# Induced attention with a leaky feed-forward: the feed-forward in 32-row TensorE tiles, four at a time

## The chip, the cores and the metric

One core of one Trainium2 chip. The metric is device microseconds (us) of one execution. Engines: TensorE (PE) multiplies, ScalarE (ACT), VectorE (DVE) and GpSimd (POOL) work elementwise, SyncE (SP) issues DMAs.

## The reference

All in float32; x is 4 x 12480 x 128, the inducing points 32 x 128.

```python
scale = 1.0 / np.sqrt(C)                       # C = 128
def mab(q, kv):
    s = scale * (q @ kv.transpose(0, 2, 1))
    s = s - s.max(-1, keepdims=True)
    a = np.exp(s)
    a /= a.sum(-1, keepdims=True) + 1e-09
    return a @ kv
h = mab(I, x)                                  # 32 inducing points look at a batch's tokens
y = mab(x, h).reshape(49920, 128)              # each token looks at the 32 rows of h
g = y @ w_in                                   # 128 x 2048
g = np.maximum(0.01 * g, g)
out = g @ w_out                                # 2048 x 128
```

## The kernel before, in words

**Algebra.** A token's attention output is a @ h with only 32 weights a, so the first product of the feed-forward is a @ (h @ w_in): it needs a contraction over 32 rows, not 128. The leaky part is split: max(0.01 g, g) = 0.99 relu(g) + 0.01 g, and the second term is linear, a @ (h @ w_in @ w_out) times 0.01. So per batch there is an expanded weight `hws` (h @ w_in, 32 x 2048, times 0.99) and a small `m2s` (the linear part, 32 x 128).

**Precision.** TensorE runs the feed-forward on the F32R type, and each operand is split into a high part and the rest (hi, lo). The 128 rows of one first product hold the four combinations of attention weights and expanded weights, 32 rows each: `A4` has ahi, alo, ahi, alo in its row groups, `hws` hi, hi, lo, lo. The second product sums over 128 of the 2048 hidden columns and takes three matmuls: ghi by w_hi, glo by w_hi, ghi by w_lo.

**Tiles and slots.** Tokens are cut into NT = 98 tiles: 24 of 512 columns per batch, and two of 384 that hold the rests of two batches each. A tile has NF = 16 slots f, one per 128 hidden columns. A slot is `ffn_first` (one matmul into a `ph` bank, L813; the relu on ACT that gives `ghi`, L821; the subtraction on DVE that gives `glo`, L823) and `ffn_second` (three matmuls into the tile's accumulator `po`, L841). The last slot adds the linear part (L847). `ffn_first` runs LOOK = 3 slots ahead. At a tile's end `store` transposes the accumulator from PSUM to SBUF on DVE (L857), and SP issues its stores (L868).

**PSUM.** Eight banks: three for `ph` and other general work, two for accumulators and the first batch's transposes, one for `h_ps`, two for the other lanes (`aux`).

**The other lanes.** The attention of the next batch runs between the slots, a few steps per slot, in an order written by hand: `first_scores` (s_ps, L305; mx_ps, L334), `first_values` with `accumulate` (h_ps, L425), `normalise`, `expand_weights` (hw_ps, L617 for the first batch, L624 for others, whose parts SP spreads over the row groups with 16 copies), `expand_linear`, then `second` (each token's weights; its two elementwise steps on POOL, L675 and L689) and `stack`, which splits them (ahi L715 on ACT, alo L720 on POOL) and lets SP copy them into the four row groups of `A4` (L732, four copies per tile). `debt` and HEAVY keep the lanes' DVE work apart. s_ps, h_ps and the later batches' hw_ps use column tiles: four matmuls of 32 output columns each, side by side. The first two tiles take their weights from `quick` and alternate in rounds of TURN = 4 slots.

## Time and profile before

| | |
|---|---|
| time, median of 3 runs | 1618.82 us (1618.67 to 1618.82) |
| span of the profiled execution | 1616.3 us |
| what lies around the span | 2.5 us, the median less the span; the profiled execution's own time is given by its span only |
| PE busy | 1598.8 us, 99% |
| DVE busy | 1289.1 us, 80% |
| ACT busy | 1009.8 us, 62% |
| POOL busy | 99.7 us, 6% |
| HBM | 48.94 MB read, 25.56 MB written |

A line of the profile that names a group of instructions has: line of the kernel, engine, operation, what is written and read, shapes and count; then busy us and mean ns of one; then the idle time of the engine before it and what ended it. Matmul durations overlap, since they are pipelined; the distance from start to start tells their price. A matmul in plain F32 makes two records.

### The profile page before, as it was taken

The page shows a single profiled execution, that of the slowest core. Times are in us where ns is not written, and L with a number is a line of the kernel's source. Part 1 is how long each engine was busy: PE and PEld are TensorE (multiplying, and loading weights), DVE is VectorE, ACT ScalarE, POOL GpSimd, SP SyncE. Part 2 cuts the span into 40 slices and gives each one's busy share as a digit, 9 for nine tenths or more (in the row PEclk, how much of TensorE's full clock was granted, in tenths as well). Part 3 has the DMA queues.
Part 4 walks back from the last instruction along what each step waited for, and adds up shares of the span by engine and source line. Part 5 has one row for each costly group of instructions (what it writes and reads, how often), then busy time and mean ns, then how long its engine had stood idle before and what let it go on. Part 6 is the DMA issues. An engine that isn't in the chain of part 4 may idle for free.

```text
span 1616.3 us, 22589 instructions
## 1 busy us (share of the span) xinstructions
PE 1598.8 (99%) x7967; PEld 1256.3 (78%) x7967; DVE 1289.1 (80%) x2245; ACT 1009.8 (62%) x1770; POOL 99.7 (6%) x100
## 2 busy tenths in 40 slices
PE   7999999999999999999999999999999999999998
PEld 5677777777778777777777777777777788888886
DVE  6778878877888888787878888877878777777776
ACT  6566666656666666566666666656666666666665
POOL 2110010000100100000011000000101000000000
PEclk9999999999999999999999999999999999999999
DMA  7142233532334245421224244531211111211211
GB/s 264 24 106 47 56 83 72 102 71 45 66 66 77 49 86 108 96 65 39 43 47 94 50 78 102 110 73 39 61 29 35 35 30 40 43 24 41 43 22 20
DMA packets 401313, 104.21 MB, mean 64 GB/s; under 512 B 372368, under 2 KB 374832, under 8 KB 401200
## 3 DMA queue, kind: packets, MB, share of 16 engines
q1 hardware_dynamic: 400096, 102.62, 30.6%
q8 instruction: 63, 1.03, 0.3%
q14 instruction: 50, 0.41, 0.1%
q10 hardware_dynamic: 1104, 0.15, 0.1%
HBM read 48.94 MB, written 25.56 MB: 46 GB/s over the span
## 4 chain that ended last, share of the span: by engine, by line
PE 97%; DMA 1%; DVE 1%; SPq 0%; ACT 0%; issue 0%; DVEq 0%; ACTq 0%
PE po L841 67%; PE ph L813 23%; PE s_ps L305 3%; PE po L847 1%; PE h_ps L425 1%; DMA xr<-in_x_dram 1%; DMA raw<-in_moe_w_in_dram 1%; PE w_ps L259 0%; SPq L513 0%; PE mx_ps L334 0%; PE hw_ps L617 0%; PE hw_ps L624 0%; PE xT_ps L538 0%; DVE glo L823 0%; PE m_ps L648 0%
## 5 line engine op out<-in xcount | busy, mean ns | idle before, releaser
L823 DVE SCALAR_TENSOR_TENSOR glo<-ph,ghi 128x512 fp32r<-128x512 f32 (+1 forms) x1568 | 1051.8, 681 | 300.1 <-ACT ghi L821 294.6
L821 ACT ACTIVATE ghi<-ph 128x512 fp32r<-128x512 f32 (+1 forms) x1568 | 933.9, 597 | 571.1 <-PE ph L813 569.4
L813 PE MATMUL ph<-A,hws 128*128 128x512 f32 (+1 forms) x1600 | 623.1, 393 | 1.5 <-DVE glo L823 1.5
L841 PE MATMUL po<-ghi,w_hi 128*128 128x512 f32 (+1 forms) x1568 | 618.1, 394 | 0.0
L841 PE MATMUL po<-glo,w_hi 128*128 128x512 f32 (+1 forms) x1568 | 616.8, 393 | 0.0
L841 PE MATMUL po<-ghi,w_lo 128*128 128x512 f32 (+1 forms) x1568 | 613.4, 391 | 0.0
L813 PEld LDWEIGHTS ph<-A,hws 128*128 128x128 f32 x1600 | 299.9, 188 | 92.1 <-DVE glo L823 14.7
L841 PEld LDWEIGHTS po<-ghi,w_lo 128*128 128x128 f32 x1568 | 294.3, 188 | 70.0
L841 PEld LDWEIGHTS po<-glo,w_hi 128*128 128x128 f32 x1568 | 294.4, 188 | 66.4
L841 PEld LDWEIGHTS po<-ghi,w_hi 128*128 128x128 f32 x1568 | 294.4, 188 | 61.1 <-issue 0.2
L720 POOL TENSOR_TENSOR alo<-aT,ahi 128x512 fp32r<-128x512 f32 x24 | 31.2, 1298 | 704.6 <-ACT ahi L715 701.9
L857 DVE STREAM_TRANSPOSE osb<-po 128x512 f32<-128x512 f32 (+1 forms) x98 | 68.9, 703 | 1.7 <-PE po L847 1.7
L675 POOL TENSOR_TENSOR y<-y,mx 128x512 f32<-128x512 f32 (+1 forms) x27 | 25.4, 940 | 458.3 <-DVE mx L673 458.3
L406 DVE STREAM_TRANSPOSE xT<-xc 128x512 f32<-128x512 f32 x72 | 50.5, 702 | 0.0
L847 PE MATMUL po<-A,m2s 128*128 128x512 f32 (+1 forms) x100 | 38.6, 389 | 0.0
L689 POOL TENSOR_TENSOR y<-y,sm 128x512 f32<-128x512 f32 (+1 forms) x27 | 25.4, 939 | 186.6 <-DVE sm L687 103.0
L425 PEld LDWEIGHTS h_ps<-xr,ay 128*32 128x32 f32 (+1 forms) x784 | 22.0, 110 | 12.8 <-issue 12.1
L425 PE MATMUL h_ps<-xr,ay 128*32 128x128 f32 (+1 forms) x784 | 27.2, 274 | 0.4 <-DVE zg L356 0.3
L305 PE MATMUL s_ps<-xT,indT 128*32 128x512 f32 x192 | 26.3, 622 | 1.2 <-ACT xT L544 1.2
L305 PE MATMUL s_ps<-xT,hT 128*32 128x512 f32 x192 | 25.6, 605 | 0.0
L317 DVE TENSOR_SCALAR_CACHE_REDUCE e<-s_ps 128x512 f32<-128x512 f32 (+1 forms) x28 | 17.1, 611 | 8.0 <-PE s_ps L305 7.7
L847 PEld LDWEIGHTS po<-A,m2s 128*128 128x128 f32 x100 | 18.7, 187 | 4.3
(111 smaller groups left out, 385.9 us busy)
## 6 DMA issues: line engine op xcount, KB each, us to landing
xr<-in_x_dram SPq DMA_DIRECT2D x96, 256.0 KB, 4.5
out_dram<-osb SPq DMA_DIRECT2D x382, 64.0 KB, 2.2
xc<-in_x_dram SPq DMA_DIRECT2D x288, 64.0 KB, 2.7
A<-ahi SPq DMA_DIRECT2D x188, 64.0 KB, 2.0
A<-alo SPq DMA_DIRECT2D x188, 64.0 KB, 2.0
raw<-in_moe_w_in_dram SPq DMA_DIRECT2D x4, 512.0 KB, 6.6
raw<-in_moe_w_out_dram SPq DMA_DIRECT2D x4, 512.0 KB, 7.2
hws<-hwhi SPq DMA_DIRECT2D x24, 64.0 KB, 2.0
```

The lines of the kernel that those rows point to most:

```text
L305: nc.tensor.matmul(dst, lhsT, rhs, start=True, stop=True)
L406: nc.vector.transpose(t[:, j, :], blk.rearrange("p n c -> p (n c)"))
L425: nc.tensor.matmul(hp[32 * k : 32 * k + 32, :C], ay[:rows, 4 * q + k, :], xb[:rows, k, :], start=(q == 0), stop=(4 * q + 4 >= K), tile_pos ...
L675: eng.tensor_tensor(out=yv, in0=yv, in1=mx[:rows, :K].unsqueeze(2).broadcast_to([rows, K, M]), op=ALU.subtract,)
L689: eng.tensor_tensor(out=yv, in0=yv, in1=smv.unsqueeze(2).broadcast_to([rows, K, M]), op=ALU.mult)
L720: (eng or nc.gpsimd).tensor_tensor(out=alo[sl], in0=aT.pop((b, g))[: 32 * J, :], in1=ahi[sl].bitcast(F32), op=ALU.subtract,)
L813: nc.tensor.matmul(ph[:, o : o + w], hw[b][1][:, f * P : (f + 1) * P], A4[t][:, o : o + w], start=True, stop=True,)
L821: nc.scalar.activation(ghi[:, :n], ph[:, :n], AF.Relu)
L823: nc.vector.scalar_tensor_tensor(out=glo[:, :n], in0=ph[:, :n], scalar=0.0, in1=ghi[:, :n].bitcast(F32), op0=ALU.max, op1=ALU.subtract,)
L841: nc.tensor.matmul(po[:, :n], w[:, f, :], r[:, :n], start=(f == 0 and r is ghi and w is w_hi), stop=False)
L847: nc.tensor.matmul(po[:, o : o + w], hw[b][2], a4[:, o : o + w], start=False, stop=(o + w == n),)
L857: nc.vector.transpose(osb[:, :n], po[:, :n])
```

## The change

In a middle phase, from tile 2 to the last but one, every matmul of the feed-forward is cut into quarters of 32 rows, each in its own row group of the array and into a PSUM bank of its own. Four generators, `row_group(0)` to `row_group(3)`, take turns, one quarter matmul each.

- A slot's first product is now three quarters (hi by hi, lo by hi, hi by lo) in row group f % 4, after one another into one `ph` bank. `A4` holds ahi and alo in two planes, each copied into all four row groups (eight copies per tile); the expanded weights stay as `expand_weights` leaves them, hidden columns f in row group f % 4, so their spreading by copies goes. The linear part takes three quarters in three of the row groups.
- A second product's three matmuls become twelve quarters, three in each row group. Each row group has its own accumulator bank, and runs LAG = 1 slot behind the one before.
- `gather` adds the four partial sums: ACT copies those of row groups 0 and 2 into SBUF, DVE adds 1 and 3 to them, POOL adds the two. `store` transposes the sum from SBUF.
- Where f % 4 is 3 (FAR), the relu goes to SBUF on ACT, and POOL makes `ghi` (a copy) and `glo` (a subtraction); its first product runs eight slots ahead, the others four. DVE's `glo` is emitted LATER = 4 turns after the relu.
- The eight banks are one pool (`bank`, `done`); in the middle phase the one that is expected free first is taken. A4_BUFS goes from 6 to 3 (of twice the size), XR from 16 to 9, the output buffers from 3 to 2.
- The lanes yield ON_PE ahead of their matmuls and are let go together by `cluster`; in the first four slots of a tile (QUIET) no lane but the stores moves. HEAVY is 2.
- The first two tiles and the last go as before with a full-array second product; their first products are four at a time, in a round of four slots (`first_round`).

```diff
-    HEAVY = 3
+    HEAVY = 2
+    FAR = 3
+    XB = 3
+    QUIET = range(4)
+    LATER = 4
+    FURTHER = 4
+    ON_PE = "pe"
...
-    A4_BUFS = 6
-    XR = 16
+    A4_BUFS = 3
+    XR = 9
+    GB = 7
+    AHEAD = 4
+    LAG = 1
...
-    ps_h = ctx.enter_context(tc.tile_pool(name="ps_h", bufs=LOOK, space=bass.MemoryType.PSUM))
-    ps_o = ctx.enter_context(tc.tile_pool(name="ps_o", bufs=2, space=bass.MemoryType.PSUM))
-    ps_s = ctx.enter_context(tc.tile_pool(name="ps_s", bufs=1, space=bass.MemoryType.PSUM))
-    ps_a = ctx.enter_context(tc.tile_pool(name="ps_a", bufs=2, space=bass.MemoryType.PSUM))
+    ps = ctx.enter_context(tc.tile_pool(name="ps", bufs=1, space=bass.MemoryType.PSUM))
+    banks = [ps.tile([P, TOK], F32, tag=f"bank{i}", name=f"bank{i}") for i in range(8)]
+    turns = {"gen": [0, 1, 2], "out": [3, 4], "hp": [5], "aux": [6, 7]}
+    quads = [False]
+    held, free = set(), []
+
+    def bank(kind):
+        if quads[0]:
+            if not free:
+                happen(math.inf)
+            i = free.pop(0)[1]
+        else:
+            i = next(i for i in turns[kind] if i not in held)
+            turns[kind].remove(i)
+            turns[kind].append(i)
+        held.add(i)
+        return banks[i]
+
+    turn = [0]
+
+    def done(t, later=6):
+        i = next(i for i in range(8) if banks[i] is t)
+        held.discard(i)
+        if quads[0]:
+            free.append((turn[0] + later, i))
+            free.sort()
...
         yield HEAVY
+        if b:
+            yield ON_PE
...
+        hi = sb.tile([P, TOK + P], F32R, tag="hwhi", name="hwhi", bufs=2)
+        lo = sb.tile([P, TOK + P], F32R, tag="hwlo", name="hwlo", bufs=2)
+        if b:
+            yield ON_PE
+        src_bank[0] = pw = aux_ps("hw_ps")
+        cols = w_in_sb.rearrange("p (q c k) -> p c q k", c=4, k=P)
...
-        for c in range(4):
-            for r in range(4):
-                nc.sync.dma_start(
-                    hws[32 * r : 32 * r + 32, c * TOK : (c + 1) * TOK].bitcast(F32),
-                    (hi, lo)[r // 2][32 * c : 32 * c + 32, :].bitcast(F32),
-                )
-            yield
+        split(hi[:, :TOK], lo[:, :TOK], pw, 1.0 - SLOPE)
+        hw[b][1:3] = hi, lo
+        yield HEAVY
...
+            while len(A4) >= A4_BUFS:
+                yield
+            a4 = sb.tile([P, 2, TOK], F32R, tag="A4", name="A4", bufs=A4_BUFS)
             to = 0
             for b, g, js in parts:
                 w, o = 32 * GROUPS[g][2], at[b, g]
                 for j in js:
-                    for r in range(4):
-                        nc.sync.dma_start(
-                            a4[32 * r : 32 * r + 32, to : to + w].bitcast(F32),
-                            (ahi, alo)[r % 2][32 * j : 32 * j + 32, o : o + w].bitcast(F32),
-                        )
+                    for which in range(2):
+                        for r in range(4):
+                            nc.sync.dma_start(
+                                a4[32 * r : 32 * r + 32, which, to : to + w].bitcast(F32),
+                                (ahi, alo)[which][32 * j : 32 * j + 32, o : o + w].bitcast(F32),
+                            )
                     to += w
-                yield
+                    yield
+            A4[t] = a4
...
+    def split_first(ph, t, f):
+
+        _, n = spans(t)
+        far, bufs = ("x", XB) if f % 4 == FAR else ("", GB)
+        ghi = sb.tile([P, TOK], F32R, tag="ghi" + far, name="ghi", bufs=bufs)
+        glo = sb.tile([P, TOK], F32R, tag="glo" + far, name="glo", bufs=bufs)
+        live[t, f] = (ghi, glo)
+        if quads[0] and f % 4 == FAR:
+            g = sb.tile([P, TOK], F32, tag="g", name="g", bufs=2)
+            nc.scalar.activation(g[:, :n], ph[:, :n], AF.Relu)
+            done(ph, 4)
+            nc.gpsimd.tensor_copy(ghi[:, :n], g[:, :n])
+            nc.gpsimd.tensor_tensor(
+                out=glo[:, :n], in0=g[:, :n], in1=ghi[:, :n].bitcast(F32), op=ALU.subtract
+            )
+            return
+        nc.scalar.activation(ghi[:, :n], ph[:, :n], AF.Relu)
+
+        def rest():
+            nc.vector.scalar_tensor_tensor(
+                out=glo[:, :n],
+                in0=ph[:, :n],
+                scalar=0.0,
+                in1=ghi[:, :n].bitcast(F32),
+                op0=ALU.max,
+                op1=ALU.subtract,
+            )
+            done(ph, 4)
+
+        if quads[0]:
+            events.append((turn[0] + LATER, rest))
+        else:
+            rest()
+
+    events = []
+
+    def happen(upto):
+        while events and events[0][0] <= upto:
+            events.pop(0)[1]()
+
+    def quarter(dst, w, x, r, start, stop):
+        nc.tensor.matmul(
+            dst, w[32 * r : 32 * r + 32], x[32 * r : 32 * r + 32],
+            start=start, stop=stop, tile_position=(32 * r, 0),
+        )
+
...
+    def ffn_first(t, f):
+
         parts, n = spans(t)
+        r, c = f % 4, f // 4 * P
         ph = gen_ps("ph")
         for b, o, w in parts:
-            nc.tensor.matmul(
-                ph[:, o : o + w],
-                hw[b][1][:, f * P : (f + 1) * P],
-                A4[t][:, o : o + w],
-                start=True,
-                stop=True,
-            )
-        ghi = sb.tile([P, TOK], F32R, tag="ghi", name="ghi", bufs=LOOK + 2)
-        nc.scalar.activation(ghi[:, :n], ph[:, :n], AF.Relu)
-        glo = sb.tile([P, TOK], F32R, tag="glo", name="glo", bufs=LOOK + 2)
-        nc.vector.scalar_tensor_tensor(
-            out=glo[:, :n],
-            in0=ph[:, :n],
-            scalar=0.0,
-            in1=ghi[:, :n].bitcast(F32),
-            op0=ALU.max,
-            op1=ALU.subtract,
-        )
-        live[u] = (ghi, glo)
-
-    def ffn_second(u):
-        t, f = slots[u]
+            for k in range(3):
+                wt, a = hw[b][1 + k % 2][:, c : c + P], A4[t][:, k // 2, o : o + w]
+                quarter(ph[:, o : o + w], wt, a, r, k == 0, k == 2)
+                if o + w == n:
+                    yield
+        split_first(ph, t, f)
+
+    def ffn_second(t, f):
+
         parts, n = spans(t)
-        ghi, glo = live.pop(u)
+        ghi, glo = live.pop((t, f))
         if f == 0:
-            accs[t] = ps_o.tile([P, TOK], F32, tag="po", name="po")
+            accs[t] = bank("out")
         po = accs[t]
-        for w, r in ((w_hi, ghi), (w_hi, glo), (w_lo, ghi)):
+        for w, r in ((w_hi, ghi), (w_lo, ghi), (w_hi, glo)):
             nc.tensor.matmul(
                 po[:, :n], w[:, f, :], r[:, :n], start=(f == 0 and r is ghi and w is w_hi), stop=False
             )
-        if f == NF - 1:
-            a4 = A4.pop(t)
-            for b, o, w in parts:
+
...
+    def store(t, total, summed):
+        if summed:
+            yield from idle(3)
+        osb = sb.tile([P, TOK], F32, tag="osb", name="osb", bufs=2)
+        nc.vector.transpose(osb[:, :n], total[:, :n])
+        if summed:
+            unsaved.remove(t)
+        else:
+            done(total)
...
+        def cluster(least):
+            for lane in (values, scores, seconds):
+                for _ in range(2):
+                    if lane and id(lane) in waiting and clock[0] - waiting[id(lane)] >= least:
+                        step(lane, True)
+
+        def next_slot(f=NF):
+            clock[0] += 1
+            debt[0] = max(0, debt[0] - (f in QUIET))
+            if f in QUIET:
+                if f >= 3:
+                    step(stores)
+                return
+            others(clock[0])
+            ages = [clock[0] - a for a in waiting.values()]
+            if ages and (max(ages) >= 10 or len(ages) > 1 and min(ages) >= 3):
+                cluster(2)
+
+        work = [(t, f) for t in range(QUICK, NT - 1) for f in range(NF)]
+
+        def row_group(r):
+
+            todo = []
+            for i, (t, f) in enumerate(work):
+                if f % 4 == r:
+                    todo.append((i - AHEAD - FURTHER * (r == FAR), 0, "first", t, f))
+                todo.append((i + LAG * r, 1, "second", t, f))
+                if r != t % 4 and f == (3 if t > QUICK + 3 else NF - 1):
+                    todo.append((i + LAG * r + 0.5, 2, "linear", t, (r - t) % 4 - 1))
+            todo.sort()
+            left = {}
+            for due_at, _, kind, t, f in todo:
+                while due_at < 8 and turn[0] < (due_at + AHEAD) * 3.75 - 1:
+                    yield
+                parts, n = spans(t)
+                if kind == "first":
+                    if f == 0:
+                        begin(t)
+                    waits = 0
+                    while t not in A4 or any(hw[b][1] is None for b, _, _ in parts):
+                        next_slot()
+                        waits += 1
+                        assert waits < 500, (t, A4.keys(), waiting)
+                    yield from ffn_first(t, f)
+                elif kind == "second":
+                    if f == 0:
+                        accs[t, r] = bank("out")
+                        left[t] = NF + (r != t % 4)
+                    po = accs[t, r]
+                    ghi, glo = live[t, f]
+                    left[t] -= 1
+                    for k, (w, x) in enumerate(((w_hi, ghi), (w_lo, ghi), (w_hi, glo))):
+                        quarter(
+                            po[:, :n], w[:, f, :], x[:, :n], r,
+                            f == 0 and k == 0, not left[t] and k == 2,
+                        )
+                        yield
+                    if r == 3:
+                        del live[t, f]
+                    if r == 0:
+                        next_slot(f)
+                else:
+                    for b, _, _ in parts:
+                        assert hw[b][3]
+                    left[t] -= 1
+                    for b, o, w in parts:
+                        quarter(
+                            accs[t, r][:, o : o + w], hw[b][1 + f % 2][:, TOK:],
+                            A4[t][:, f // 2, o : o + w], r, False, not left[t] and o + w == n,
+                        )
+                    yield
+                if t in left and not left[t]:
+                    del left[t]
+                    gather(t, r)
+
+        def gather(t, r):
+            _, n = spans(t)
+            po = accs.pop((t, r))
+            if r % 2 == 0:
+                while unsaved:
+                    step(stores)
+                parts_of[t, r] = part = sb.tile([P, TOK], F32, tag="part", name="part", bufs=2)
+                nc.scalar.copy(part[:, :n], po[:, :n])
+            else:
+                part = parts_of[t, r - 1]
+                nc.vector.tensor_tensor(out=part[:, :n], in0=po[:, :n], in1=part[:, :n], op=ALU.add)
+            done(po)
+            if r == 3:
+                total, part = parts_of.pop((t, 0)), parts_of.pop((t, 2))
+                nc.gpsimd.tensor_tensor(out=total[:, :n], in0=total[:, :n], in1=part[:, :n], op=ALU.add)
+                unsaved.append(t)
+                stores.append(store(t, total, True))
+                del A4[t]
+
+        streams = [row_group(r) for r in range(4)]
+        while streams:
+            streams = [m for m in streams if next(m, StopIteration) is not StopIteration]
+            turn[0] += 1
+            happen(turn[0])
...
```

More of the change, by code (lines that the diff above doesn't have):

```diff
@@ L608, in expand_weights @@
+    src_bank = [None]
     def expand_weights(b):
         hT = hw[b][0]
-        hws = sb.tile([P, DFF], F32R, tag="hws", name="hws", bufs=2)
-        hw[b][1] = hws
-        if b == 0:
-            for c in range(4):
-                sl = slice(c * TOK, (c + 1) * TOK)
-                pw = ps_s.tile([P, TOK], F32, tag="hp", name="hw_ps")
-                nc.tensor.matmul(pw, hT, w_in_sb[:, sl], start=True, stop=True)
-                yield
-                yield from split(hws[:, sl], pw, TOK, 1.0 - SLOPE)
-                yield from idle(3 if c else 1)
-            return
@@ L654, in second, with expand_linear @@
+        hw[b][1:3] = hi, lo
+        yield HEAVY
+    def expand_linear(b):
+        hT, hi, lo, _ = hw[b]
+        if b:
+            yield ON_PE
+        src_bank[0] = pw = aux_ps("m2_ps")
+        nc.tensor.matmul(pw[:, :P], hT, w12, start=True, stop=True)
+        split(hi[:, TOK:], lo[:, TOK:], pw[:, :P], 1.0)
+        hw[b][3] = True
+        yield
     def second(b, g, eng=None):
@@ L702, in stack @@
     def stack(tiles_, eng=None):
-        while len(A4) + len(tiles_) > A4_BUFS or not all(s[:2] in aT for t in tiles_ for s in t[1]):
+        while not all(s[:2] in aT for t in tiles_ for s in t[1]):
             yield
@@ L752, in quick @@
         nc.vector.tensor_reduce(out=mx, in_=sv, op=ALU.max, axis=AX.X)
[L753 removed]
+        y = sb.tile([P, 4, M], F32, tag=("ahi", "alo")[t], name="qy", bufs=1)
         nc.vector.tensor_tensor(
@@ L766, in quick @@
         yield
-        pa = ps_o.tile([P, TOK], F32, tag="po", name="a4_ps")
+        pa = bank("out")
         for c in range(4):
@@ L886, in idle, with step @@
             yield
-    def step(lane):
-        if lane:
-            got = next(lane[0], StopIteration)
-            if got is StopIteration:
-                lane.pop(0)
-            elif got:
-                debt[0] += got
+    waiting = {}
+    clock = [0]
+    def step(lane, on_pe=False):
+        if not lane or (id(lane) in waiting and not on_pe):
+            return
+        waiting.pop(id(lane), None)
+        got = next(lane[0], StopIteration)
+        while got is ON_PE and not quads[0]:
+            got = next(lane[0], StopIteration)
+        if got is StopIteration:
+            lane.pop(0)
+        elif got is ON_PE:
+            waiting[id(lane)] = clock[0]
+        elif got:
+            debt[0] += got
     def after_h(b):
@@ L923, in induced_attention_then_leaky_ffn, with first_round @@
         for lane in (
-            one, weights, two, one, weights, one, two, weights, one, one, two, two, one, two,
+            one, weights, two, one, one, two, one, one, two, two, one, two,
         ):
             step(lane)
-        ffn_first(0)
-        ffn_first(1)
+        def first_round(t, f0):
+            made = [ffn_first(t, f0 + k) for k in range(TURN)]
+            while made:
+                made = [m for m in made if next(m, StopIteration) is not StopIteration]
+            happen(math.inf)
+        first_round(*rounds[0])
         step(two)
-        ffn_first(2)
         stacks[0] = stacks[0][QUICK:]
@@ L968, in induced_attention_then_leaky_ffn @@
                     step(values)
-                    if b + 1 in hw and not had:
-                        seconds += [second(b + 1, g) for g in [0, 1, RG, 2, 3, 4, 5]]
+            for b in hw:
+                if b not in known:
+                    known.add(b)
+                    seconds.extend(second(b, g) for g in [0, 1, RG, 2, 3, 4, 5])
+        begin(0)
+        u = 0
+        for i, (t, f0) in enumerate(rounds):
+            if i + 1 < len(rounds):
+                first_round(*rounds[i + 1])
+            for f in range(f0, f0 + TURN):
+                ffn_second(t, f)
+                if f == NF - 1:
+                    linear_part(t)
+                    stores.append(store(t, accs.pop(t), False))
+                others(u)
+                u += 1
@@ new lines, in induced_attention_then_leaky_ffn @@
+        while weights or linear:
+            step(weights)
+            step(linear)
+        for lane in (stores,):
+            while len(lane) > 1 or held & {3, 4}:
+                step(lane)
+        quads[0] = True
+        free.extend((0, i) for i in [*range(3), 5, 6, 7, 3, 4] if i not in held)
+        clock[0] = u
+        def cluster(least):
[3 more added lines that the diff above has]
+                        step(lane, True)
@@ L971, in induced_attention_then_leaky_ffn @@
+        linear_part(t)
+        stores.append(store(t, accs.pop(t), False))
         for gen in stores:
```

171 lines of the change are left out of this document (79 added, 92 removed).

## The prediction

> **What bounds the kernel now.** I read the page first: the share of each engine and the chain that ended last.
>
> ```profile
> span 1616.3 us, 22589 instructions
> PE 1598.8 (99%) x7967; PEld 1256.3 (78%) x7967; DVE 1289.1 (80%) x2245; ACT 1009.8 (62%) x1770; POOL 99.7 (6%) x100
> PEclk9999999999999999999999999999999999999999
> PE 97%; DMA 1%; DVE 1%; SPq 0%; ACT 0%; issue 0%; DVEq 0%; ACTq 0%
> L823 DVE SCALAR_TENSOR_TENSOR glo<-ph,ghi 128x512 fp32r<-128x512 f32 (+1 forms) x1568 | 1051.8, 681 | 300.1 <-ACT ghi L821 294.6
> L821 ACT ACTIVATE ghi<-ph 128x512 fp32r<-128x512 f32 (+1 forms) x1568 | 933.9, 597 | 571.1 <-PE ph L813 569.4
> L813 PE MATMUL ph<-A,hws 128*128 128x512 f32 (+1 forms) x1600 | 623.1, 393 | 1.5 <-DVE glo L823 1.5
> ```
>
> TensorE is the bound: 97% of the chain, granted clock full throughout, and the feed-forward's own matmul (L813) waited 1.5 us in all. ACT and DVE are the ones that wait (571 and 300 us). A matmul's 393 ns overlaps its neighbours, so its price is read from start to start, in the timeline of one slot (one of a tile's 16 f):
>
> ```profile
> 803.80 0.40 PE L813 MATMUL ph<-A,hws 128*128 128x512 f32 x1
> 803.80 0.19 PEld L841 LDWEIGHTS po<-ghi,w_hi 128*128 128x128 f32 x1
> 804.03 0.40 PE L841 MATMUL po<-ghi,w_hi 128*128 128x512 f32 x1
> 804.23 0.60 ACT L821 ACTIVATE ghi<-ph 128x512 fp32r<-128x512 f32 x1 [0.33 <-PE ph L813]
> 804.27 0.39 PE L841 MATMUL po<-glo,w_hi 128*128 128x512 f32 x1
> 804.50 0.39 PE L841 MATMUL po<-ghi,w_lo 128*128 128x512 f32 x1
> 804.73 0.39 PE L813 MATMUL ph<-A,hws 128*128 128x512 f32 x1
> 804.87 0.69 DVE L823 SCALAR_TENSOR_TENSOR glo<-ph,ghi 128x512 fp32r<-128x512 f32 x1 [0.24 <-ACT ghi L821]
> ```
>
> Four matmuls in 0.93 us, 0.23 each. The last stage, where hardly anything but the feed-forward runs, gives it exactly; in the chain each tile ends on such a row:
>
> ```profile
> 1324.56 0.70 PE po L841 x3
> ...
> 1595.76 0.70 PE po L841 x3
> ```
>
> Eighteen tiles in 271.2 us: 15.07 us a tile, over 65 matmuls (16 times four, and one linear part) 0.2318 us.
>
> **The change on TensorE.** A slot's first product becomes three products of 32 rows, and the three second products become twelve; a tile's linear part becomes three. That is 16 x 15 + 3 = 243 quarter matmuls, four at a time 60.75 rounds. Whether a round costs one matmul's 0.2318 us is the heart of the forecast. No 32-row tile is in this trace; the nearest rows are the 32-column tiles of an excursion, which also go four at a time:
>
> ```profile
> 264.68 0.40 PE L841 MATMUL po<-ghi,w_lo 128*128 128x512 f32 x1
> 265.00 1.06 PE L305 MATMUL s_ps<-xT,indT 128*32 128x512 f32 x8
> 265.89 1.06 PE L425 MATMUL h_ps<-xr,ay 128*32 128x128 f32 x32
> 265.89 0.79 PEld L425 LDWEIGHTS h_ps<-xr,ay 128*32 128x32 f32 x28 [0.30 <-issue]
> 266.87 0.50 PE L813 MATMUL ph<-A,hws 128*128 128x512 f32 x1
> 267.21 0.39 PE L841 MATMUL po<-ghi,w_hi 128*128 128x512 f32 x1
> L425 PEld LDWEIGHTS h_ps<-xr,ay 128*32 128x32 f32 (+1 forms) x784 | 22.0, 110 | 12.8 <-issue 12.1
> 57.26 1.09 PEld L259 LDWEIGHTS w_ps<-wraw,winT 128*128 128x128 f32 x8
> 57.49 1.05 PE L259 MATMUL w_ps<-wraw,winT 128*128 128x128 f32 x8
> 58.30 0.48 PE L813 MATMUL ph<-A,hws 128*128 128x512 f32 x1
> ```
>
> Eight full-array records of 128 columns (L259) take 0.81 us until the next matmul starts, 0.10 each. Thirty-two quarter records of the same length (L425) take 0.98 us, change of shape included: 0.12 for a round of four. So the four run beside each other, and so do their weight loads: 28 of 110 ns, 3.1 us together, lie within 0.79. Issue is no limit either: 0.98/32 = 31 ns a pair, where a round has 58. I take 0.2318 us a round. Above it the bound is 0.32 (the step into another shape, 264.68 to 265.00, paid in every round); below, a round is no faster than the one matmul it copies. A tile takes 60.75 x 0.2318 = 14.08 us, 0.99 less. 95 tiles of 98 go this way: **-93.6**. The first two and the last compute only their first products in quarters: 12 rounds, 48 full matmuls and 3 lone quarters make 63 steps of 0.2318, 0.46 us less each, against eight changes of shape of about 0.1 each: **+1**.
>
> The Trainium skill, "TensorE: Matmul & The Clock Gate", Part 3 (Measured speedup vs the span model), puts four row tiles of 512 columns at 3.07 times one, not 4. By that a round would cost 4/3.07 x 0.2318 = 0.302 us, a tile 18.3, and the kernel about 1940 us, an estimate. The column tiles above do not bear it out in steady state, and no run here shows row tiles yet.
>
> **Excursions.** Entering another shape costs 0.32 - 0.23 = 0.09 us, leaving it 0.34 - 0.23 = 0.11 (266.87 to 267.21), with some drain besides: 0.3 together. They are paid already around s_ps and h_ps. What is full-array work now pays them newly:
>
> ```profile
> L334 PE MATMUL mx_ps<-rd,e 128*128 128x4 f32 x56 | 8.1, 214 | 1.0 <-DVE rd L329 1.0
> L617 PE MATMUL hw_ps<-w_in_sb,hT 128*128 128x512 f32 x8 | 4.2, 602 | 0.0
> ```
>
> 28 mx_ps (two records each), batch 0's seven before the new phase, and with them z_ps, hT_ps and m_ps, some 30 times, 9 us; gathering the lanes' work into clusters behind ON_PE saves some of the old ones. **+5**, bounds -6 and +9.
>
> **The other engines, by stage.**
>
> ```profile
> 100.00:400.00 300.00, 300.00 (x1516) 233.59 (x1515) 245.38 (x437) 186.36 (x329) 16.50 (x16) 1.00 0.34 68
> 400.00:700.00 300.00, 299.60 (x1482) 236.26 (x1481) 246.45 (x439) 188.40 (x334) 19.26 (x20) 1.00 0.39 78
> 700.00:1000.00 300.00, 300.00 (x1459) 233.70 (x1458) 243.39 (x424) 186.60 (x324) 18.38 (x18) 1.00 0.33 67
> 1000.00:1300.00 300.00, 300.00 (x1455) 235.20 (x1454) 241.01 (x406) 188.90 (x332) 20.30 (x21) 1.00 0.26 53
> L720 POOL TENSOR_TENSOR alo<-aT,ahi 128x512 fp32r<-128x512 f32 x24 | 31.2, 1298 | 704.6 <-ACT ahi L715 701.9
> L675 POOL TENSOR_TENSOR y<-y,mx 128x512 f32<-128x512 f32 x23 | 24.2, 1053 | 394.1 <-DVE mx L673 394.1
> L148 POOL TENSOR_TENSOR w_in_sb<-cv_a,cv_t 128x512 f32<-128x512 f32 x4 | 5.7, 1430 | 23.5 <-DVE cv_t L144 23.5
> ```
>
> The columns after the stretch are PE, PEld, DVE, ACT and POOL busy. The 1200 us hold about 74 tiles of 16.2 us: DVE 13.2 us a tile, ACT 10.1, POOL 1.0.
> - DVE loses a quarter of its glo (4 x 0.68), gains two additions of partial sums, priced like a glo: 11.8 us. It stays below the new period of 15.2: nothing on the path.
> - ACT keeps its 16 relus and gains two copies of a partial sum, priced like a ghi (0.60): 11.3.
> - POOL, nearly idle now, takes every fourth f: a copy (bounds 0.29, the 96x64 y, and 1.43, w_in_sb; I take y's 1.05, the row with the least second input) and a subtraction (alo, 1.30), four times a tile, and the final addition (1.30): 11.7 us with its own, and with 1.43 for all nine 13.9. Below the period even in the last stage (14.1), so hidden; the eight slots (7 us) of lead cover 0.43 + 0.60 + 2.35 and a y queued ahead. If that cover were gone, POOL would set the period.
> - The store is emitted three slots later; its transpose now reads SBUF after POOL's addition. Only the last tile's tail shows, and that tile keeps the old way: 0.
> - SP: a tile's A4 takes eight copies instead of four, one weight spread of 48 copies goes.
>
> ```profile
> L675 POOL TENSOR_TENSOR y<-y,mx 96x64 f32<-96x64 f32 x4 | 1.2, 291 | 64.1 <-DVE mx L673 64.1
> L732 SPq DMA_DIRECT2D A<-ahi x212: 507/582/1368, 81.6 to 1533.9; - x106
> SPq L868 <- DVE glo L823: 480.1, 81, 14.6
> ```
>
> 424 - 48 = 376 more issues of 0.58 us are 218 us of SP's queue. A store that waits for its transpose (480 us now, no load of its own) holds the copies behind it, but three A4 buffers let a tile's copies be issued more than a tile ahead: 0. Only tile 2, the first of the new phase, has no such lead: up to 8 x 0.58 + 2, in the next item.
> - Hand-overs: the four streams start and end once, each a chain of ph, ghi, glo (0.43 + 0.60 + 0.69 and two more rounds, 2.2 us), and the old phase's stores are drained first: **+6** (bounds 2 and 13). Batch 0's four full hw_ps products (L617, 4.2 us busy with their overlaps) become one set of column tiles (0.89, as s_ps): **-1**, bounds 0 and -3.
>
> **What is late next: PSUM banks.** The four partial sums hold four of eight banks, and each keeps its old one while it is read out: 0.43 + 0.60 + 0.3 of queueing, 1.3 us in 14.1, together 4.4 banks. A ph bank is held two rounds longer than now: 0.46 + 0.43 + 0.60 + 0.04 + 0.69 + 0.3 = 2.5 us (1.5 where POOL takes over): 9.0 bank-us in 3.48, 2.6 banks. Mean 7.0 of 8, 7.3 with the other lanes'. But where a tile changes, four banks turn over one slot (0.87 us) apart and 1.5 more are out for about 4 us: 5.5 + 2.6 = 8.1. There TensorE waits, all four streams with it, since its queue is in order. Bounds: nothing, and one whole read-out (1.3 us); nearer the lower end, as the excess is 0.1 of a bank, I take 0.35 us a tile: **+33** (0 to 124).
>
> Sum: -93.6 + 1 + 5 + 6 - 1 + 33 = -49.6, from the span of 1616.3 to 1566.7. The runs shown have a median of 1618.82, 2.5 above that span; so 1569 us.
>
> **Rivals.**
> 1. No wait for banks (15%): other lanes are kept off a tile's first four slots, and releases fall into place. Against it speaks the 8.1. 1536 us.
> 2. The waits eat it (15%): every tile change waits for a read-out that stands in ACT's or DVE's queue behind two relus or glos. ACT is at 74%, DVE at 78% of the new period, which speaks for queueing; today's 1.5 us of waits at 81% DVE speak against. 1.3 us a tile give 1660; it decides from (93.6 - 11)/95 = 0.87 us a tile. Slower in most of it. The Trainium skill, "TensorEngine Tiling (Array Packing)", PSUM Bottleneck, warns the same way: tiling speeds up TensorE, not the read-out.
> 3. Rounds drain (6%): 32-row tiles write four banks at once, which column tiles never do; if each round drained as the change of shape does, 0.32 a round, a tile takes 19.4 and the kernel about 2040. It decides from (93.6 - 44)/95/60.75 = 9 ns a round. The skill's 3.07 would be this case, at its 0.302.
> 4. Weight loads of row tiles go one after another (4%): 128 columns at 0.10 (L259), four in 0.40, a round takes 0.40: a tile 24.3, about 2500. Against it: the 28 loads in 0.79, though of 32 columns each.
>
> **How the numbers follow.** The forecast has 60%, with a range of its own of 1540 to 1605. The change that a measurement here can tell from none is about 0.2% (3 us). Faster: 60 + 15 = 75%; same 4%, slower 11% out of rival 2, with 3 and 4 slower 21%. The range reaches down to 1520 (rival 1 with excursions at their lower bound), up to 1650 into rival 2; outside are 3, 4 and the end of 2, about 17%.
>
> **What will show it.** In the last stage, tiles 14.1 to 14.5 us apart; within a slot, row tiles starting in groups of four 0.23 us apart. Starts 0.30 or 0.40 apart would be rivals 3 or 4. Idle time of TensorE behind ACT's copies of partial sums or DVE's additions, bunched at f = 0 to 3, is the bank term; idle time behind POOL would mean that its price was wrong, and waits for A4's copies that SP was.

## The result: slower by 3.4%, where 3% faster was forecast

| | before | after |
|---|---|---|
| median | 1618.82 us (1618.67 to 1618.83) | 1674.28 us (1673.30 to 1675.05) |
| ratio to before, 95% interval | | 1.0342 [1.0328, 1.0357] |
| profiled execution | span 1616.3 us | 1674.81 us, span 1672.7 us |

The forecast was 1569 us, with a range of 1520 to 1650. The page after, from its shares of engines, its slices, its chain and its groups of instructions:

```profile
span 1672.7 us, 60122 instructions
PE 1562.8 (93%) x25047; PEld 1353.4 (81%) x25047; DVE 1163.7 (70%) x2046; ACT 1066.9 (64%) x1957; POOL 941.7 (56%) x963
PE   8999999999966899999996999999999598999997
PEclk9899999999977999999998999999999799999998
PE 79%; SPq 11%; DMA 3%; DVE 3%; issue 2%; POOL 1%; ACT 1%; ACTq 0%; DVEq 0%; POOLq 0%
L874 PE MATMUL bank<-ghi,w_hi 32*128 32x512 f32 x6080 | 1295.8, 394 | 0.6 <-DVE part L1157 0.4
L874 PE MATMUL bank<-A,hwhi 32*128 32x512 f32 (+1 forms) x3394 | 1136.0, 394 | 68.1 <-ACT g L842 62.4
L844 POOL CAST ghi<-g 128x512 fp32r<-128x512 f32 (+1 forms) x384 | 234.1, 610 | 407.1 <-ACT g L842 339.2
L845 POOL TENSOR_TENSOR glo<-g,ghi 128x512 fp32r<-128x512 f32 (+1 forms) x384 | 495.7, 1291 | 30.7
```

Before, TensorE was busy in every slice, at full clock, and was 97% of the chain. Now its row falls to 6 or 5 in three places, PEclk falls there too, and 11% of the chain is SP's queue. The matmuls themselves are as fast as forecast. In the timeline of a stretch late in the kernel, four quarter matmuls start together, with four weight loads of 0.18 us beside them (one is shown), and the next matmuls start 0.23 us later:

```profile
1403.27 0.39 PE L874 MATMUL bank<-ghi,w_lo 32*128 32x512 f32 x1
1403.27 0.39 PE L874 MATMUL bank<-ghi,w_hi 32*128 32x512 f32 x1
1403.27 0.39 PE L874 MATMUL bank<-A,hwhi 32*128 32x512 f32 x1
1403.27 0.39 PE L874 MATMUL bank<-ghi,w_lo 32*128 32x512 f32 x1
1403.27 0.18 PEld L874 LDWEIGHTS bank<-glo,w_hi 32*128 32x128 f32 x1
1403.50 0.39 PE L874 MATMUL bank<-glo,w_hi 32*128 32x512 f32 x2
```

What was lost lies in seven holes of more than 3 us between 100 and 1640 us. The next view gives each engine's busy time in the longest two (columns: stretch, length, then PE, PEld, DVE, ACT and POOL busy, granted clock, DMA share, GB/s) and its sum over all seven (at 465.0, 502.4, 578.8, 906.4, 1107.8, 1316.4 and 1389.3 us):

```profile
502.40:519.10 16.70, 0.04 (x3) 0.00 (x0) 0.00 (x0) 1.66 (x4) 0.00 (x0) 0.57 0.16 27
1316.40:1334.20 17.80, 0.02 (x4) 0.03 (x4) 0.77 (x2) 1.92 (x4) 0.00 (x0) 0.62 0.16 26
sum 82.40, PE 0.22 PEld 0.11 DVE 0.77 ACT 9.20 POOL 0.02; mean PE 0.03 PEld 0.02 DVE 0.11 ACT 1.31 POOL 0.00
```

The computing engines do next to nothing, for 82 us together (ACT, the busiest, works 9 of them). Behind each hole TensorE works, but not at full clock (the same view for the 14 us behind each; the last but two columns give the clock):

```profile
479.30:493.00 13.70, 13.69 (x176) 10.01 (x180) 8.65 (x15) 7.66 (x14) 6.85 (x9) 0.81 0.22 39
519.10:533.00 13.90, 13.88 (x183) 12.63 (x187) 11.47 (x20) 9.11 (x17) 11.04 (x11) 0.78 0.41 77
589.00:603.00 14.00, 13.41 (x192) 10.44 (x196) 9.36 (x19) 8.08 (x16) 7.51 (x8) 0.83 0.67 147
920.30:934.00 13.70, 13.31 (x175) 11.60 (x179) 9.43 (x18) 8.94 (x17) 10.26 (x11) 0.84 0.34 69
1111.20:1125.00 13.80, 13.67 (x212) 10.15 (x216) 8.42 (x16) 8.03 (x15) 8.10 (x8) 0.88 0.60 139
1334.20:1348.00 13.80, 13.80 (x206) 11.51 (x210) 10.36 (x17) 8.77 (x17) 9.13 (x9) 0.87 0.25 52
1395.40:1409.00 13.60, 13.60 (x189) 10.96 (x193) 9.11 (x15) 8.81 (x16) 9.15 (x10) 0.86 0.32 65
```

One less the clock, times the length, sums to 15.6 us. So holes and clock account for 98 us. Without them the kernel would take some 1576, close to the forecast. What makes the holes is in the list of waits (us in total, times, longest) and in the timeline around the longest hole:

```profile
ACT ahi L735 <- DMA A<-ahi: 93.9, 8, 18.9
POOL alo L740 <- DMA A<-alo: 64.4, 6, 19.1
PE bank L874 <- ACT g L842: 62.4, 6, 16.7
```

```profile
1320.55 2.61 SPq L935 DMA_DIRECT2D out_dram<-osb  x4
1323.20 2.52 SPq L755 DMA_DIRECT2D A<-ahi  x4
1325.77 2.49 SPq L755 DMA_DIRECT2D A<-alo  x4
1328.31 2.49 SPq L755 DMA_DIRECT2D A<-ahi  x4
1330.84 2.49 SPq L755 DMA_DIRECT2D A<-alo  x4
1332.28 0.62 ACT L735 CAST ahi<-aT 128x512 fp32r<-128x512 f32 x1 [18.90 <-DMA A<-ahi]
1332.81 1.56 ACT L849 ACTIVATE ghi<-bank 128x512 fp32r<-128x512 f32 x3
1333.43 1.89 DVE L852 SCALAR_TENSOR_TENSOR glo<-bank,ghi 128x512 fp32r<-128x512 f32 x3 [20.37 <-ACT ghi L849]
1334.18 1.93 PE L334 MATMUL bank<-xT,hT 128*32 128x512 f32 x8 [17.83 <-DVE glo L852]
```

`stack` casts the attention weights of the next tiles into `ahi` (L735), of which there is one buffer. The cast may not overwrite it until the copies of the stack before have read it. SP issues those one behind another, about 0.62 us each, and has stores and loads among them. The cast stands at the head of ACT's queue for 18.9 us, and the relus that TensorE needs stand behind it: at 1332.81 three of them run back to back. All seven holes end this way: in each, a cast into `ahi` that had waited 4.9 to 18.9 us for the copies runs 0.9 to 1.9 us ahead of TensorE's return (at 478.4, 517.4, 587.9, 919.1, 1110.0, 1332.3 and 1394.2 us). POOL's subtraction into `alo`, also of one buffer, waits in the same way, 64.4 us in all. The Trainium skill, "TensorE: Matmul & The Clock Gate", Part 1, says that ACT's queue is a strict first-in first-out; here the relus are not moved past the waiting cast.

Before, `ahi` had one buffer too, yet its cast waited for no DMA. Its row in the groups of the kernel before:

```profile
L715 ACT CAST ahi<-aT 128x512 fp32r<-128x512 f32 x24 | 14.7, 614 | 0.6 <-DVE aT L698 0.4
```

The old `stack` began with `while len(A4) + len(tiles_) > A4_BUFS or not all(...)`: it waited for room for all its tiles, then cast, then put the copies of one tile after another into SP's queue, with no further wait for room. The new one casts first and copies tile by tile, whenever one of three `A4` comes free. So the last copy that reads `ahi` is issued tiles later, often behind other work of SP. Its timeline of the changed kernel ahead of the hole at 465 us:

```profile
437.20 20.41 SPq L320 DMA_DIRECT2D xc<-in_x_dram  x28
457.65 3.36 SPq L310 DMA_DIRECT2D xr<-in_x_dram  x5
461.11 2.44 SPq L755 DMA_DIRECT2D A<-ahi  x4
463.60 2.50 SPq L755 DMA_DIRECT2D A<-alo  x4
```

These 28 loads of the next batch are 20 us of issues. A tile that holds the rests of two batches takes 48 small copies, 30 us, and 24 small stores (the same view, ahead of the hole at 578.8):

```profile
560.41 17.73 SPq L935 DMA_DIRECT2D out_dram<-osb  x24
```

### The profile page after: what moved, and what is told of

It is laid out like the page before. It is cut to its first block, busy times and chain, and to the rows that moved or that the text cites. A ratio compares the mean times of both kernels' runs of the same rounds, so it can differ in the third digit from the quotient of the medians.

```text
span 1672.7 us, 60122 instructions
## 1 busy us (share of the span) xinstructions
PE 1562.8 (93%) x25047; PEld 1353.4 (81%) x25047; DVE 1163.7 (70%) x2046; ACT 1066.9 (64%) x1957; POOL 941.7 (56%) x963
## 4 chain that ended last, share of the span: by engine, by line
PE 79%; SPq 11%; DMA 3%; DVE 3%; issue 2%; POOL 1%; ACT 1%; ACTq 0%; DVEq 0%; POOLq 0%
PE bank L874 72%; SPq L755 4%; SPq L320 3%; SPq L935 3%; PE bank L334 2%; PE bank L900 2%; PE bank L458 1%; DMA xr<-in_x_dram 1%; DVE glo L852 1%; DMA A<-ahi 1%; POOL glo L845 1%; DMA raw<-in_moe_w_in_dram 1%; ACT ghi L849 0%; DMA A<-alo 0%; PE bank L365 0%
## 5 line engine op out<-in xcount | busy, mean ns | idle before, releaser
L874 PE MATMUL bank<-ghi,w_hi 32*128 32x512 f32 x6080 | 1295.8, 394 | 0.6 <-DVE part L1157 0.4
L874 PE MATMUL bank<-glo,w_hi 32*128 32x512 f32 x6080 | 1295.1, 393 | 0.2 <-DVE glo L852 0.2
L874 PE MATMUL bank<-ghi,w_lo 32*128 32x512 f32 x6080 | 1294.5, 394 | 0.0
L874 PE MATMUL bank<-A,hwhi 32*128 32x512 f32 (+1 forms) x3394 | 1136.0, 394 | 68.1 <-ACT g L842 62.4
L852 DVE SCALAR_TENSOR_TENSOR glo<-bank,ghi 128x512 fp32r<-128x512 f32 x1184 | 796.1, 681 | 350.7 <-ACT ghi L849 344.4
L849 ACT ACTIVATE ghi<-bank 128x512 fp32r<-128x512 f32 x1184 | 701.6, 598 | 296.1 <-PE bank L874 269.8
L874 PEld LDWEIGHTS bank<-ghi,w_hi 32*128 32x128 f32 x6080 | 847.3, 185 | 46.5 <-issue 17.6
L874 PEld LDWEIGHTS bank<-glo,w_hi 32*128 32x128 f32 x6080 | 850.0, 185 | 27.3 <-DVE glo L852 0.6
L874 PEld LDWEIGHTS bank<-ghi,w_lo 32*128 32x128 f32 x6080 | 849.4, 185 | 25.0
L874 PEld LDWEIGHTS bank<-A,hwhi 32*128 32x128 f32 x3394 | 586.2, 185 | 115.1 <-ACT g L842 66.6
L874 PE MATMUL bank<-A,hwlo 32*128 32x512 f32 (+1 forms) x1697 | 642.5, 391 | 0.0
L845 POOL TENSOR_TENSOR glo<-g,ghi 128x512 fp32r<-128x512 f32 (+1 forms) x384 | 495.7, 1291 | 30.7
L874 PEld LDWEIGHTS bank<-A,hwlo 32*128 32x128 f32 x1697 | 307.4, 185 | 7.6
L740 POOL TENSOR_TENSOR alo<-aT,ahi 128x512 fp32r<-128x512 f32 x24 | 31.0, 1291 | 83.0 <-DMA A<-alo 45.8
L735 ACT CAST ahi<-aT 128x512 fp32r<-128x512 f32 x24 | 14.8, 615 | 88.7 <-DMA A<-ahi 78.2
```

The costliest lines, as they stand in the source:

```text
L845: nc.gpsimd.tensor_tensor(out=glo[:, :n], in0=g[:, :n], in1=ghi[:, :n].bitcast(F32), op=ALU.subtract)
L849: nc.scalar.activation(ghi[:, :n], ph[:, :n], AF.Relu)
L852: nc.vector.scalar_tensor_tensor(out=glo[:, :n], in0=ph[:, :n], scalar=0.0, in1=ghi[:, :n].bitcast(F32), op0=ALU.max, op1=ALU.subtract,)
L874: nc.tensor.matmul(dst, w[32 * r : 32 * r + 32], x[32 * r : 32 * r + 32], start=start, stop=stop, tile_position=(32 * r, 0),)
```

## The experiments

**The copies taken away.** Is it the copies at all, or the row tiles and their banks? This kernel leaves the copies out, and every tile multiplies the first tile's `A4`.

```diff
-            a4 = sb.tile([P, 2, TOK], ...); its eight nc.sync.dma_start
-            A4[t] = a4
+            A4[t] = fixed[0]
```

> The 848 copies of A4 are left out; every tile multiplies the first tile's A4, which stays in SBUF (the output is then not the reference's for the other tiles). All else of the changed kernel runs as it is, the lanes, the casts ahi and alo and the order of instructions included. Theory S (SP's queue delivers A4 too late: six holes of 6 to 18 us on TensorE, 79 us together, and half clock behind each): no hole over 2 us between 100 and 1640 us, last stage unchanged at 14.15 us a tile, time 1560 to 1575 us. Rival L (the lanes are behind in the order of instructions, so that aT and the stacks themselves come late): holes stay where they are, since a tile still waits for its stack in program order; 1660 to 1675. Rival C (the clock falls by itself): half clock stays, 1630 or more.

1573.8 us, 0.9717 [0.9701, 0.9733]. Its page, from the slices and the chain:

```profile
PE   7899999999999999999999999999999999999997
PEclk9899999999999999999999999999999999999998
PE 95%; DVE 3%; ACT 1%; DMA 0%; issue 0%; SPq 0%; DVEq 0%; ACTq 0%
```

No hole between 100 and 1540 us. So the loss hangs on the copies: the difference to the changed kernel is 100.5 us, close to the 98 found above. Rivals L and C are out: the lanes run here as they did, and the clock stays full.

**More lead, fewer issues.** A fourth A4 buffer (room from one `ghi`/`glo` pair); one copy per row group for both planes, 376 of full size instead of 752; and both. (Where an edit takes room, here and below, a line that lists buffers to borrow for the first loads and a tile of `quick` change with it; they are not shown.)

```diff
-    A4_BUFS = 3
-    GB = 7
+    A4_BUFS = 4
+    GB = 6
...
```

```diff
-                    for which in range(2):
-                        for r in range(4): nc.sync.dma_start(a4[32 * r : ..., which, ...], (ahi, alo)[which][...])
+                    for r in range(4): nc.sync.dma_start(a4[32 * r : ..., :, ...], both[32 * j : ..., :, ...])
```

> A4_BUFS from 3 to 4, so that copies may be issued one tile (14 us) earlier; paid for with ghi and glo buffers, 7 to 6. SP issues as much as before. Theory S: the holes at the starts of batches (14.3, 13.9 and 3.4 us) go, those around the tiles of two batches (16.7, 10.2, 17.8, 6.1) shrink by up to 14 each: 1595 to 1620 us. Rival A (ACT is what waits: ahi has one buffer, and its cast stands in ACT's queue until the copies of the stack before are done): the holes at 502 and 1316 us stay, 1625 to 1640. Rival L: 1660 to 1680.

> ahi and alo become two planes of one tile, so that one copy fills both planes of a row group: four copies of A4 per tile instead of eight, 24 instead of 48 small ones for a tile of two batches, the same bytes, lead as it was (three A4). Theory S (what counts is the number of issues at 0.6 us, not bytes): the holes at 502 and 1316 us, behind 48 issues of 30 us together, shrink by about 15 us to under 4; those at the starts of batches, behind 33 issues of x, shrink only by the 2.5 to 5 us of A4's own copies, to about 10; time 1600 to 1625 us. If bytes counted: no change, 1665 to 1680.

> Both: four A4 and one copy for both planes. Theory S: under 15 us of holes in all, 1560 to 1585 us, faster than the kernel before by about 3%. Rival A: as S here, since fewer issues free ahi sooner. Rival L: 1655 or more.

1662.46 (1.0278 [1.0255, 1.0301]), 1649.35 (1.0180 [1.0156, 1.0204]) and 1627.21 us (1.0049 [1.0032, 1.0065]): 11.8, 24.9 and 47.1 us less than the changed kernel, and all three less of a gain than expected. (The first lies in the range of rival L, which the run without copies has ruled out.) With four buffers, the holes at 465 and 502 (14.3 and 16.7 us) became one of 32.2 at 487; its timeline ends on

```profile
517.36 0.62 ACT L735 CAST ahi<-aT 128x512 fp32r<-128x512 f32 x1 [34.42 <-DMA A<-ahi]
```

The same backlog now met one cast. With the planes, the two holes at the tile of two batches shrank by about 12 us each, where about 15 were expected, those at the starts of batches by little, as expected (465: 14.3 to 12.4; 906: 13.9 to 12.6; about 10 forecast), and those behind the 24 small stores not at all (578.8: 10.2 to 10.1; 1389.3: 6.1 to 6.8). So the number of issues of A4's copies explains a part of the holes only.

**SP's loads spread.** In `first_scores`, eight steps of rest after each of the first three blocks of loads:

```diff
             more()
-        yield from idle(4)
+            yield from idle(8)
```

> One edit to the changed kernel: first_scores asks for its first three blocks of x eight steps apart instead of at once, so that the 28 loads (20 us of issues) that open a batch no longer stand in one piece ahead of A4's copies. Three A4, eight copies per tile as before. Theory S: the holes at the starts of batches (465, 906 us: 14.3 and 13.9) fall under 3 us, those at the tiles of two batches (502, 578, 1316, 1389) stay; with the half clock behind them that is 35 to 45 us: 1628 to 1642. If the lanes' lateness were the cause (rival L), later loads make it worse: 1680 or more.

1692.36 us, 1.0457 [1.0442, 1.0473]: slower, against the expectation. The hole at 906 shrank to 3.7 us and one of 6.6 at 445 stands in place of that at 465, but the ones around the two-batch tiles grew (14.1 and 17.6 us at 516 and 533; 24.4 instead of 17.8 at 1327). SP's timeline gives two reasons at the first of these tiles: SP stands idle for 10.5 us, 502.2 to 512.7, until the tile's own cast, which is late in the order of instructions, and one block of eight loads (5.3 us) falls among its copies. Which weighs more was not measured. So lanes that run later do cost time, as rival L foresaw for this edit; that does not make them the cause in the changed kernel.

**The cast freed.** The edit goes at the cast alone and leaves SP's issues as they are: two buffers for `ahi` and `alo`.

```diff
-    GB = 7
+    GB = 6
...
-        ahi = sb.tile([P, TOK], F32R, tag="ahi", name="ahi", bufs=1)
-        alo = sb.tile([P, TOK], F32R, tag="alo", name="alo", bufs=1)
+        ahi = sb.tile([P, TOK], F32R, tag="ahi", name="ahi", bufs=2)
+        alo = sb.tile([P, TOK], F32R, tag="alo", name="alo", bufs=2)
```

> ahi and alo get two buffers each (room from ghi and glo, 7 to 6), so that ACT's cast for the next stack need not wait for the 48 small copies of a tile of two batches. Rival A (ACT, in order, stands at that cast and holds the relus behind it): the holes at 502 and 1316 us (16.7 and 17.8) go, all others stay: 1625 to 1640. Theory S in its plain form (TensorE lacks A4 itself): these holes stay or shrink little, since the next tile's copies stand behind the 48 all the same: 1660 to 1675.

1611.7 us, 0.9962 [0.9949, 0.9974]: 62.6 us less than the changed kernel, more than expected, and not in the places expected: five of the seven holes went, those at the starts of batches among them, but one of 15.1 us stayed at 503 and one of 5.7 at 1281. From its groups and its waits:

```profile
L735 ACT CAST ahi<-aT 128x512 fp32r<-128x512 f32 x24 | 14.7, 612 | 1.2 <-DVE aT L718 1.2
```

```profile
PE bank L874 <- DMA A<-ahi: 23.5, 5, 15.1
```

The cast waits for no DMA any more. SP issues the copies no sooner than before: at the first hole the copies of one tile stood at 474.29 and 476.80 in the changed kernel and here, in SP's timeline, at

```profile
476.19 3.75 SPq L755 DMA_DIRECT2D A<-ahi  x4
479.99 2.49 SPq L755 DMA_DIRECT2D A<-alo  x4
```

and there is no hole. Those copies were in time for TensorE; only the cast that waited for them was not. In the two holes left TensorE itself waits for a tile's copies, at the tile of two batches. `ahi` and `alo` were doubled together, so this run does not part ACT's wait from POOL's.

**The cast put off.** One line, `yield from idle(9)`, ahead of the cast.

> One line in the changed kernel: a stack waits nine of its steps (about nine slots, 8 us) ahead of the cast into ahi, so that ACT reaches it when the copies of the stack before are further on. No buffer is added, nothing else moves. Theory A (ACT, in order, stands at that cast and holds the relus): most holes go, the long ones at the tiles of two batches (30 us of issues) shrink by 8 us: 1615 to 1640 us, from 1674. If the gain with two buffers came from anything else in that edit: 1665 to 1680.

1651.64 us, 1.0211 [1.0194, 1.0228]: a miss. Waiting casts still take 51.7 us, and nine slots later the stack's copies are themselves late: `PE bank L875 <- DMA A<-ahi` is 29.6 us in its list of waits. This delay is no substitute for a buffer.

**Both causes mended.** Three combinations. The first: four A4, planes, spread loads, and the two-batch tile behind twelve full tiles of its batch instead of four (PAIR_AT). The second: three A4, planes in two buffers, spread loads, PAIR_AT 12. The third is the second without the spreading:

```diff
+        both = sb.tile([P, 2, TOK], F32R, tag="ahl", name="ahl", bufs=2)
...
-    PAIR_AT = 4
+    PAIR_AT = 12
```

> Four A4, one copy for both planes, loads eight steps apart, and the tile of two batches moved from fifth to thirteenth of its batch (PAIR_AT 12), away from the loads that open it. Theory S: no hole over 3 us between 100 and 1590 us; 1574 to 1590, faster than the kernel before by 2 to 3%. If a hole stays at the moved tile, it is rival A's, some 15 us each.

> As the run before it, but the room goes to a second buffer for the planes of ahi and alo, and A4 stays at three. If the lead of A4 decides: holes of 3 to 8 us at the starts of batches come back, 1590 to 1610. If ACT's cast decides: none at the moved tile, 1574 to 1590.

> Planes, a second buffer for them, the tile of two batches thirteenth; the loads of x at once, as in the changed kernel. Theory A with S for the rest: no hole over 3 us between 100 and 1560 us, 1570 to 1580 us, 2.4 to 3% faster than the kernel before. If the spread loads were not what made the last hole of 8 us (441 us) of the run with two planes and spread loads: it stays, 1585 to 1590.

1623.52 (1.0028 [1.0018, 1.0039]), 1587.5 (0.9806 [0.9791, 0.9820]) and 1576.4 us (0.9743 [0.9728, 0.9757]). The first misses its 1574 to 1590: more lead, fewer issues, spread loads and the moved tile together do not do without the second buffer, and casts still wait 33.2 us. The second, inside the range for ACT's cast, has one hole over 3 us left, 8.3 us at 441.5 us, where TensorE waits for a tile's copies, as was expected if the lead of A4 decides. The third, as expected, has none. It is the fastest of those that copy, 2.6% faster than before, and 2.6 us from the kernel without copies. Its page:

```profile
span 1575.5 us, 59851 instructions
PE   7899999999999999999999999999999999999997
PE 92%; SPq 3%; DMA 2%; DVE 2%; issue 0%; ACT 0%; DVEq 0%; ACTq 0%
```

**The suspected part alone, in the kernel before.** No row tiles; only three A4 buffers and the new order in `stack`; then the same with two `ahi` and `alo`:

```diff
-    A4_BUFS = 6
+    A4_BUFS = 3
...
-        while len(A4) + len(tiles_) > A4_BUFS or not all(s[:2] in aT for t in tiles_ for s in t[1]):
+        while not all(s[:2] in aT for t in tiles_ for s in t[1]):
             yield
...
-            A4[t] = a4 = sb.tile([P, TOK], F32R, tag="A4", name="A4", bufs=A4_BUFS)
+            while len(A4) >= A4_BUFS:
+                yield
+            a4 = sb.tile([P, TOK], F32R, tag="A4", name="A4", bufs=A4_BUFS)
```

> The kernel before, full-array matmuls and all, with two things of the change alone: three A4 buffers instead of six, and a stack that casts first and then copies tile by tile as an A4 comes free. Four copies per tile, as before. Theory A: ACT stands at casts behind copies that SP issues late, at the tiles of two batches (24 small copies, 15 us) and behind the loads that open a batch: 10 us holes on TensorE and half clock behind them, 1640 to 1670. If the holes need the 32-row tiles or eight copies: 1617 to 1622.

> The same with two buffers for ahi and alo. Theory A: back to 1617 to 1625. If three A4 buffers are too few by themselves (TensorE without A4): as without the second buffers, 1640 or more.

1722.49 us, 1.0645 [1.0629, 1.0661], and 1618.32 us, 1.0000 [0.9991, 1.0010]. The row of the cast in the groups of the one, then of the other:

```profile
L715 ACT CAST ahi<-aT 128x512 fp32r<-128x512 f32 x24 | 14.9, 621 | 90.2 <-DMA A<-ahi 89.2 <-DVE aT L698 0.9
```

```profile
L715 ACT CAST ahi<-aT 128x512 fp32r<-128x512 f32 x24 | 14.7, 614 | 1.0 <-DVE aT L698 0.9
```

With three buffers and the new order the old kernel loses 104 us, more than expected and about what the changed kernel lost to the copies; with one more buffer each for `ahi` and `alo` it loses nothing. The row tiles are not needed for the loss, nor is the doubled number of copies. Nor is POOL's wait: here POOL makes no `ghi` or `glo`, and it is ACT's cast that holds the relus. Three buffers and the new order were not taken apart.

## Why the prediction was wrong

**The step that failed** is the one on SP: "three A4 buffers let a tile's copies be issued more than a tile ahead: 0". It asked who waits for the copies' result, and answered for TensorE alone. It did not ask who waits for the copies to have read their source. The order of `stack` had changed as well (cast, wait for room, copy), and with one `ahi` the next cast depends on SP's last issue. That wait is the one the change added, it stands at the head of ACT's queue, and the relus of all four streams are queued behind it. It was priced at nothing and costs 62.6 us, by the second buffers of `ahi` and `alo` alone. The remaining 35.3 us (1611.7 to 1576.4) went with the planes and the later two-batch tile. Some 23 of them are holes of 2.1, 15.1 and 5.7 us (at 501, 503 and 1281) in which TensorE waits for a tile's copies: there the failed sentence was wrong as it stands, since the copies were not ahead. The rest, half clock behind these holes among it, was not split. The prediction had named waits for A4's copies as the sign that its price for SP was wrong. The trace shows them, most of them on ACT instead of TensorE.

**The terms of the sum** can be read from the kernel without copies. By count, TensorE's feed-forward fell from 6404 matmuls to 23331 quarters and 153 whole ones or lone quarters, 418 rounds or 96.9 us less, the narrow matmuls of the two-batch tiles counted as whole ones (forecast, 93.6 less and 1 more: 92.6). Its span fell by 43.9, so 53.0 us of other time came in, where 43 were forecast, but in other places:

- Banks, +33: over-sized. In the tile view of the last stage of the changed kernel, the final additions go from tile to tile in 226.7/16 = 14.17 us, 0.09 above the 14.08 of the rounds:

```profile
L1161 POOL TENSOR_TENSOR part<-part x17: 1291/1297/1300, 1406.6 to 1633.3; 128x512 f32<-128x512 f32 x17
```

  That is 9 us over 95 tiles, if the other stages are like the last. The 8.1 banks reckoned for a tile's change did not become a wait of any size: in the whole changed kernel, L874's waits are 0.4 us for DVE's additions and none for ACT's copies of partial sums. Rival 1 was nearly right here.
- Excursions, +5: under-sized. Between 100 and 1300 us the kernel without copies has

```profile
100.00:1300.00 1200.00, 1132.58 (x19040) 1002.36 (x19044) 1.00 0.27 50
```

  of L867, its quarter matmuls: 4760 rounds, 1103.4 us, 96.6 for all else. The kernel before, counted the same way, has 4879 matmuls, 1131.0 us, and 69.0 for all else. Of the 27.6 us more, 7 are the 0.09 us of 78 tiles; some 20 are left, above the bound of 9 for the excursions. About 1.7 of these are half clock at 105 us; that the rest is the excursions' was not isolated.
- Hand-overs, +6: under-sized. The other 25 us came before 100 and after 1300 us, where the upper bound was 13. A part of it is half clock: in the kernel without copies the granted clock is 0.51 from 47 to 54 us, 0.52 from 57 to 64.1 and again 0.52 near the end, some 10 us lost together, where the kernel before keeps full clock until TensorE is done. The end shows how it comes: two short holes, and behind them the last tile, a full-array one, at half clock (the stretches of 1544.9 to 1546.7, 1547.9 to 1550.2, and then)

```profile
1550.20:1556.00 5.80, 5.75 (x16) 4.13 (x20) 0.62 (x1) 0.00 (x0) 1.50 (x2) 0.52 0.30 45
```

- hw_ps, -1: not measured by itself.

That the kernel without copies, at 1573.8, came near the forecast of 1569 is therefore partly luck: 24 us too much for banks stood against too little elsewhere.

**What was right.** The round of four costs one matmul's price (0.233 us in the last stage, 14.17 over 60.75 rounds), and its four weight loads go abreast, so rivals 3 and 4 fall. The Trainium skill's 3.07 in "TensorE: Matmul & The Clock Gate", Part 3, and the 1940 us by it fall with them: a round here does four. DVE, ACT and POOL stay below the period, 74, 68 and 60% busy in the kernel without copies; POOL's copy takes 0.61 us, not 1.05. Rival 2's time, 1660, came close for a reason that it did not have: TensorE's waits are not at tile changes, and the read-outs of PSUM do not make them. That the time was near it is luck.

## What to carry to other kernels

When a change moves a producer ahead of the wait for room, follow its single buffer in both directions: who waits for the data, and who waits for the last reader to be done. If that reader is a DMA on a busy queue, and the writer shares an in-order engine with the critical work, try one more buffer first: here it gave 62.6 us for two tiles of memory, where saving half of the copies' issues gave 24.9 and more lead 11.8. And price a sum's terms from a run that isolates them before trusting that a total has come out right.

## What the runs showed of the hardware that was not expected

- A hole costs more than its length: after seven holes of 3.4 to 17.8 us the clock fell to a mean of 0.78 to 0.88 over the next 14 us, 15.6 us on top of 82. The Trainium skill, "TensorE: Matmul & The Clock Gate", Part 1, speaks of half clock after an idle window of about 3.4 us, regained after as long a busy one; the hole of 3.4 us here agrees, with (1 - 0.88) x 13.8 x 2 = 3.3 us at half clock behind it. But 3.4 us is no threshold for a single hole. In the kernel before with three buffers and the new order, a hole of 2.3 us at 1003.2 is followed by 0.62 over 4.5 us. In the kernel without copies the clock is 0.51 from 47 us on with no gap over 1.5 us near it. And in the fastest kernel with copies, holes of 2.9 and 2.2 us (467.4 and 856.2) leave it full.
- Row tiles with an accumulating bank each run at the full fourfold rate in the last stage, 0.233 us a round against 0.232 for one full-array matmul, with no drain seen between rounds.
- POOL's plain copy of 128x512 takes 610 ns, under half of its two-operand subtraction (1291).
